# R loaded for two chunks at once in the first eight batches and turned apart from V, products of ones 512 wide, and a new written order

## The chip, the cores and the metric

The kernel runs on one core of a Trainium2 chip. The metric is device time in microseconds (us). A core has TensorE (PE, with its weight loads PEld), VectorE (DVE), ScalarE (ACT), GpSimd (POOL) and SyncE (SP), which here only issues transfers; 16 DMA engines carry these.

## The reference

Inputs r, k, v, w, a, b are fp32 of 4 x 8 x 768 x 40 (batch, head, time, head dimension). A linear recurrence runs over time for each of the 32 heads, and its output goes through a two-layer block:

```python
for t in range(S):
    y[:, :, t] = np.einsum('bhd,bhde->bhe', rt, state)
    Sa = np.einsum('bhde,bhe->bhd', state, at)
    state_decay = state * wt[:, :, None, :] - np.einsum('bhd,bhe->bhde', Sa, bt)
    state = state_decay + np.einsum('bhd,bhe->bhde', vt, kt)
...
x = y.transpose(0, 2, 1, 3).reshape(B * S, H * D)      # 3072 x 320
h = x @ w_in                                           # w_in 320 x 2048
out = (np.maximum(h, 0.0) ** 2) @ w_out                # w_out 2048 x 320
```

## The kernel before

**Tiling.** Time is cut into 6 chunks of 128 steps. A "batch" m = 0..23 in the code is one chunk (c = m // 4) of one of the four input batches (bb = m % 4), all 8 heads; batches 0 to 3 are the first chunk, 4 to 7 the second. A step st = 0..47 is half of a batch, four heads. Inside a chunk the recurrence is done with products of 128 x 128; between chunks a state UZ is carried.

**One batch.** SP loads W, K, B, A, R and V, 128 times x 8 heads x 40 in fp32, 160 KB each (`load`). PE sums the logarithms of W over time (cs), ACT takes exponentials (xi, gp), and DVE or POOL multiply them into padded bf16 tiles: K and B (pk), A (pa), the last decay (gw). R and V are copied into a pad by one instruction (cv). The padded tiles are turned, so that heads lie along partitions: K and B on PE (kt, then the eviction kv), A on PE for the first eight batches (ta, at) and by a transposing DMA later (ka); R and V on PE for the first eight (rm, evicted by rv) and by a transposing DMA later (rt). Then come the products `ca` (a), masked into CN: either by one DVE multiplication with MEX, or by an ACT copy and a cut on POOL (affine select; aq and eq in the order). P collects V's share and the carried state (p), and a correction in two steps (m, k1, c, k2) gives SN (s). SN is turned (t, tv), the products `ex` are made with turned R, V and SN (e) and masked into EX in the same two ways (ev). `uy` takes output and new state (z, kb), which DVE scales (y, u). The output is turned (xt, xv) and enters the two-layer block: fr, fa, fb are products with w_in, ra and rb the rectification on ACT, q the square on POOL or DVE, o1 and o2 the products with w_out, ov the eviction, ow the store.

**The order.** Nothing is scheduled by the compiler. The string `ORDER` lists every piece of work by name and number, as `ev0.1:D` or `cs.4@f`: after the colon stands the engine, after the @ the PSUM bank. Each engine executes its own pieces in the order of the string, and so do the transfers on SP's one queue. A load's place in the string is its place in that queue; weights (wt, wo) go by POOL's queue.

**Buffers.** The loaded tiles lie in a pool with four buffers for each kind (`natp`, `AHEAD = 4`); R and V share the kind NRV. A load waits until the tile four before it has been copied.

**Products of ones.** `warm` (w.0 to w.18) writes products of a 128 x 128 tile of ones into a spare bank, 26 for w.0 and 8 for the others, 170 in all; nothing reads them.

At the end of the program a test value is read by all engines (fl), and the last two outputs are stored behind a branch.

Of the kernel before, what the change touches and what calls it, by code (L numbers as in the profile page):

```python
# [18 lines left out]
def kernel(  # L19
# [57 lines left out]
    def natural(key, m):  # L77
        if (key, m) not in nat:
            nat[key, m] = natp.tile([128, len(key), NHH, D], FP32, name=f"N{key}", tag=f"N{key}")
        return nat[key, m]  # L80

    def load(key, m):
        pair, u = SHARED.get(key, (key, 0))
        c, bb = divmod(m, NB)
        nc.sync.dma_start(  # L85
            out=natural(pair, m)[:, u],
            in_=nat_srcs[key][bb, :, c * L:(c + 1) * L, :].rearrange("h t e -> t h e"))
# [12 lines left out]
            for key, n in (("KBA", 4), ("G", 3), ("RV", 4))}  # L100
    RVs = [gl.tile([128, 2, PB, L], BF16, name=f"RV{i}") for i in range(4)]
# [6 lines left out]
    def fill(k):  # L108
# [7 lines left out]
        elif k < 16:  # L116
            key, i = (("KBA", k - 5) if k < 9 else ("G", k - 9) if k < 12 else ("RV", k - 12))
            eng.memset(pads[key][i][:] if key == "G" else pads[key][i][:, :, :, D:64], 0.0)
        elif k < 19:
            eng.memset(SNs[k - 16][:, :, :, D:64], 0.0)  # L120
        else:
            eng.memset(UZs[k - 19][:], 0.0)
# [11 lines left out]
    def warm(k, n=8):  # L134
        wu = ps.tile([128, 128], FP32, name="wu", **bank("w", k))
        for i in range(26 if k == 0 else n):
            nc.tensor.matmul(out=wu[:], lhsT=ones_b[:], rhs=ones_b[:], start=True, stop=True)
# [23 lines left out]
    def home(m):  # L161
        o = bt[m] = Batch()
        o.G, o.KB, o.RV = (pads[key][m % len(pads[key])] for key in ("G", "KBA", "RV"))
        o.RVT, o.YN = RVs[m % 4], YNs[m % 3]

# [40 lines left out]
    def b_pa(m):  # L206
        engine("pa", m).tensor_tensor(out=bt[m].KB[:, 2, :, 0:D], in0=nat.pop(("A", m))[:, 0],  # L207
                                      in1=bt[m].GP[:], op=ALU.mult)

    def b_cv(m):  # L210
        move(pick["cv", m][0], bt[m].RV[:, :, :, 0:D], nat.pop(("RV", m))[:])
# [11 lines left out]
    def b_rm(m):  # L223
        bt[m].t1 = turned(bt[m].RV, **bank("rm", m))

    def b_rv(m):
        move(pick["rv", m][0], bt[m].RVT[:], bt[m].t1[:])

    def b_rt(m):
        o = bt[m]  # L230
        nc.sync.dma_start_transpose(
            out=o.RVT[:].rearrange("p u j t -> p (u j) t"),
            in_=o.RV[:].rearrange("p u h e -> p (u h e)"))
# [4 lines left out]
    def kbt(m):  # L238
        o = bt[m]
        if not hasattr(o, "KBT"):  # L240
            o.KBT = chp.tile([128, 3, PB, L], BF16, name="KBT", tag="KBT", bufs=4)
        return o.KBT

    def b_kv(m):
        move(pick["kv", m][0], kbt(m)[:, 0:2], bt[m].t2[:])

    def b_ta(m):
        bt[m].t3 = turned(bt[m].KB, us=(2,), **bank("ta", m))

# [30 lines left out]
    def st_a_mm(st):  # L280
# [40 lines left out]
    def b_p(m):  # L321
# [3 lines left out]
        if c > 0:  # L325
            for j in range(PB):
                nc.tensor.matmul(out=P[:, j, :, 0:D], lhsT=o.KBT[:, 2, j, :],
# [73 lines left out]
    def st_ex_mm(st):  # L401
# [4 lines left out]
        for u in range(2):  # L406
            for i in range(2):
                for s in range(2):
                    lhsT = SnT[half(s), j0 + i, :] if u else o.RVT[half(s), 1, j0 + i, :]
                    nc.tensor.matmul(out=ex[s][:, i, u, :], lhsT=lhsT,  # L410
                                     rhs=o.RVT[half(s), 0, j0 + i, :],
# [18 lines left out]
    def st_z(st):  # L430
        c, o, j0, p2, SN = where(st)
        uy = uys[st] = ps.tile([128, 8 * D + PB], FP32, name="uy", **bank("z", st))
        if c > 0:
            for i in range(2):
                nc.tensor.matmul(out=cols(uy, 2 * i * D), lhsT=o.RVT[:, 0, j0 + i, :],
# [184 lines left out]
    def get_flag():  # L620
# [297 lines left out]
```

## Time and profile before

| | us |
|---|---|
| median of 3 runs | 257.62 (256.45 to 258.14) |
| the profiled execution, its time | 259.12 |
| its span, first to last instruction | 257.3 |
| granted TensorE clock, mean | 0.993 |

| engine | busy us | share of the span |
|---|---|---|
| PE | 241.3 | 94% |
| PE weight loads | 201.8 | 78% |
| DVE | 202.4 | 79% |
| ACT | 205.9 | 80% |
| POOL | 203.0 | 79% |

A profile line names the source line of kernel.py, the engine, the operation, what is written and read by the program's names, and the shape. Busy PE time counts overlapping products once and can hold short stalls. The row of slices has 40 digits, each the busy share in tenths of a fortieth of the span. "DMA share" is the mean busy share of the 16 DMA engines and can come out a little over 1. Where several helpers call one line, such as `move` (L153 on ACT, L157 on DVE), tiles tell the groups apart: RVp is the pad of R and V, RV the turned tile, KBT the turned K, B and A.

### The profile page before, as it was taken

How to read it: one execution, taken by the hardware profiler on the slowest of the kernel's cores; microseconds unless marked ns; L12 is line 12 of the kernel's file. 1: busy time of each engine (PE TensorE's matmuls, PEld its weight loads, DVE VectorE, ACT ScalarE, POOL GpSimd, SP SyncE). 2: the span in 40 equal slices, each digit the busy share in tenths (PEclk: the TensorE clock that was granted, in tenths of full speed). 3: DMA queues.
4: the chain of work that ended last, by engine and by line, in shares of the span. 5: the costliest groups of instructions: out<-in, count | busy, mean ns of one | idle time of the engine just before them, and what ended most of it. 6: DMA issues, size and time to landing. Idle time of an engine off the chain costs nothing.

```text
span 257.3 us, 9803 instructions
## 1 busy us (share of the span) xinstructions
PE 241.3 (94%) x4020; PEld 201.8 (78%) x4020; DVE 202.4 (79%) x429; ACT 205.9 (80%) x470; POOL 203.0 (79%) x231
## 2 busy tenths in 40 slices
PE   8897867999999999999999999999999997999993
PEld 7776656989888888788888788888878885787872
DVE  3887877899999889898798898879798986664440
ACT  3567989589989988978999887889989876869811
POOL 6487987779989979999998999897896993397110
PEclk9999999799999999999999999999999999999999
DMA  7999999999988989999999999989999989470011
GB/s 127 182 151 153 169 176 168 170 167 167 162 162 137 157 151 182 137 178 180 157 159 184 159 167 172 167 162 185 141 187 180 178 167 148 97 120 28 28 57 59
DMA packets 184468, 38.46 MB, mean 149 GB/s; under 512 B 180064, under 2 KB 183136, under 8 KB 184416
## 3 DMA queue, kind: packets, MB, share of 16 engines
q1 hardware_dynamic: 183072, 35.14, 80.9%
q0 software_dynamic: 1344, 2.62, 6.4%
q8 instruction: 33, 0.54, 0.9%
q14 instruction: 19, 0.16, 0.2%
HBM read 28.84 MB, written 3.93 MB: 127 GB/s over the span
## 4 chain that ended last, share of the span: by engine, by line
PE 58%; POOL 13%; DMA 12%; SPq 8%; ACT 4%; issue 2%; DVE 1%; POOLq 0%; ACTq 0%
PE hp L542 17%; SPq L85 8%; DMA NKB<-in_b_dram 6%; PE tt L218 3%; PE cs L173 3%; PE ca L287 3%; PE ex L410 3%; POOL Gt L568 3%; PE uy L456 3%; DMA NRV<-in_r_dram 2%; DMA KBT<-KBAp 2%; POOL KBAp L202 2%; PE uy L451 2%; PE P L344 2%; POOL CN L307 2%
## 5 line engine op out<-in xcount | busy, mean ns | idle before, releaser
L542 PE MATMUL hp<-XS,WIN 128*128 128x256 bf16 (+3 forms) x720 | 73.3, 255 | 0.0
L562 ACT ACTIVATE hs<-hp 128x512 bf16<-128x512 f32 x96 | 55.6, 600 | 14.5 <-PE hp L542 13.2
L542 PEld LDWEIGHTS <-WIN 128*128 128x128 bf16 (+1 forms) x720 | 49.6, 115 | 6.1 <-issue 3.6
L302 DVE TENSOR_TENSOR CN<-ca,MEX 128x512 bf16<-128x512 f32 x60 | 39.5, 683 | 8.6 <-PE ca L287 8.0
L577 PEld LDWEIGHTS <-Gt 128*128 128x128 bf16 x384 | 35.1, 97 | 12.2 <-issue 0.3
L302 DVE TENSOR_TENSOR EX<-ex,MEX 128x512 bf16<-128x512 f32 x60 | 39.8, 683 | 4.4 <-PE ex L410 4.3
L568 POOL TENSOR_TENSOR Gt<-hs 128x1024 bf16<-128x1024 bf16 x21 | 40.4, 1927 | 0.6 <-ACT hs L562 0.3
L307 POOL TENSOR_SCALAR_AFFINE_SELECT CN<-CN 128x512 bf16<-128x512 bf16 x36 | 25.1, 703 | 10.0 <-ACT CN L300 7.8
L307 POOL TENSOR_SCALAR_AFFINE_SELECT EX<-EX 128x512 bf16<-128x512 bf16 x36 | 25.0, 711 | 5.9 <-ACT EX L300 3.9
L198 POOL TENSOR_TENSOR Gp<-NW,GP 32x320 bf16<-32x320 f32 x20 | 17.6, 886 | 11.3 <-DVE osb L157 7.6
L568 DVE TENSOR_TENSOR Gt<-hs 128x1024 bf16<-128x1024 bf16 x27 | 21.7, 810 | 5.8 <-ACT hs L562 4.3
L365 ACT ACTIVATE jk<-CN 128x1024 bf16<-128x1024 bf16 x24 | 25.7, 1071 | 0.2
L300 ACT ACTIVATE CN<-ca 128x512 bf16<-128x512 f32 x36 | 21.0, 594 | 4.7 <-PE ca L287 4.5
L202 POOL TENSOR_TENSOR KBAp<-NKB,GI 128x640 bf16<-128x640 f32 x14 | 21.6, 1545 | 3.2 <-DMA NKB<-in_b_dram 2.5
L300 ACT ACTIVATE EX<-ex 128x512 bf16<-128x512 f32 x36 | 20.5, 597 | 2.8 <-PE ex L410 1.9
L287 PE MATMUL ca<-KBT 64*128 64x128 bf16 x384 | 18.2, 221 | 3.7 <-DMA KBT<-KBAp 1.7
L361 POOL TENSOR_TENSOR Cc<-x,SN 128x320 bf16<-128x320 f32 x24 | 20.1, 836 | 1.9
L456 PE MATMUL uy<-KBAp,EX 128*128 128x40 bf16 x384 | 21.3, 181 | 0.0
L207 POOL TENSOR_TENSOR KBAp<-NA,GP 128x320 bf16<-128x320 f32 x18 | 16.3, 907 | 5.6 <-DMA NA<-in_a_dram 2.9
L360 POOL TENSOR_TENSOR x<-Mc,c 128x320 f32<-128x320 bf16 x24 | 20.5, 854 | 0.3
L472 DVE TENSOR_TENSOR YN<-uy,GP 128x224 bf16<-128x224 f32 (+1 forms) x48 | 16.5, 346 | 4.4 <-PE uy L456 4.4
L456 PEld LDWEIGHTS <-EX 128*128 128x128 bf16 x384 | 17.9, 96 | 0.9 <-issue 0.3
(151 smaller groups left out, 623.0 us busy)
## 6 DMA issues: line engine op xcount, KB each, us to landing
NW<-in_w_dram SPq DMA_DIRECT2D x24, 160.0 KB, 3.8
NA<-in_a_dram SPq DMA_DIRECT2D x24, 160.0 KB, 4.0
NKB<-in_k_dram SPq DMA_DIRECT2D x24, 160.0 KB, 3.9
NKB<-in_b_dram SPq DMA_DIRECT2D x24, 160.0 KB, 4.3
NRV<-in_v_dram SPq DMA_DIRECT2D x24, 160.0 KB, 4.0
NRV<-in_r_dram SPq DMA_DIRECT2D x24, 160.0 KB, 3.9
out_dram<-osb SPq DMA_DIRECT2D x24, 160.0 KB, 3.4
WOUT<-in_moe_w_out_dram POOLq DMA_DIRECT2D x2, 640.0 KB, 6.6
```

The source lines that it names most:

```text
L85: nc.sync.dma_start(out=natural(pair, m)[:, u], in_=nat_srcs[key][bb, :, c * L:(c + 1) * L, :].rearrange("h t e -> t h e"))
L202: engine("pk", m).tensor_tensor(out=bt[m].KB[:, 0:2, :, 0:D], in0=nat.pop(("KB", m))[:], op=ALU.mult, in1=bt[m].GI[:].rearrange("p (u h) e ...
L287: nc.tensor.matmul(out=ca[s][:, i, u, :], lhsT=o.KBT[half(s), u, j0 + i, :], rhs=o.KBT[half(s), 2, j0 + i, :], start=(i == 0 and u == 0), ...
L300: nc.scalar.activation(out=out, in_=in_[:], func=ACTF.Copy)
L302: nc.vector.tensor_tensor(out=out, in0=in_[:], op=ALU.mult, in1=MEX[:].rearrange("p (i u) x -> p i u x", u=2))
L307: nc.gpsimd.affine_select(out=t_, in_=t_, pattern=[[0, 2], [0, 2], [1, L]], compare_op=ALU.is_gt, fill=0.0, base=0, channel_multiplier=-1)
L365: nc.scalar.activation(out=jk[:], in_=CNs[m, "b"][:].rearrange("p x i s u t -> p (x i s) u t")[:, :, 1, :], func=ACTF.Square, accum_out=AC ...
L456: nc.tensor.matmul(out=uy[:, (2 * i + s) * D:(2 * i + s + 1) * D], lhsT=EXs[st][:, i, s, u, :], rhs=o.KB[:, u, 2 * (j0 + i) + s, 0:D], sta ...
L542: nc.tensor.matmul(out=o.hp[u][:, i], lhsT=inner(g, rows, j), rhs=XSs[o.c][rows, g, o.bs, :], start=(o.begun[u] == 1), stop=(o.begun[u] > ...
L562: nc.scalar.activation(out=o.hs[:, u], func=ACTF.Relu, in_=o.hp[u][:].rearrange("p j a b -> p (j a b)"))
L568: engine("q", n).tensor_tensor(out=o.Gt[:, o.j0:o.j0 + 2 * o.per].rearrange("p j a b -> p (j a b)"), in0=hs, in1=hs, op=ALU.mult)
L577: nc.tensor.matmul(out=ops[n][:], rhs=WOUT[:, j, :], lhsT=Gts[h][:, b_, j, :] if h in SPLIT else Gts[h][:, j, b_, :], start=(j == 0), stop ...
```

## The change

**R in pairs.** For batches 0 to 7 R is loaded by four transfers instead of eight (lR.0 to lR.3). One takes 256 steps of one input batch, that is both chunks; partition p gets steps 2p and 2p + 1, which lie side by side in memory: 320 bytes in one piece instead of 160. The tile takes a buffer of the kind NRV, and V of these batches takes another of its own. R is copied into the pads of two batches by one instruction (cr), V alone by cv. On PE each R turn (rn) covers two pairs of heads for both chunks; it is an ordinary product with the identity into fp32, and its eviction (rv) reads the steps apart and writes two batches' turned R, the second chunk's into a fourth plane of the turned tile. V is turned by itself (vm, vv).

**A's pad.** A moves from the pad of K and B (now KBp) to the pad of R and V (now RVAp), and turned A from KBT to a plane of RV. From batch 8 on A has a transfer of its own (aa), R and V theirs (rt); in the last four batches K and B are turned by a transfer of 8 blocks (ka), where one of 12 blocks held A too.

**Products of ones.** 7 for w.0 and 2 for the others, each with 512 columns: 43 in all.

**Order.** The whole string is written anew, with other engines for many pieces.

```diff
+    def paired(m):
+        return ("cr", m - m // NB % 2 * NB) in pick
     def load(key, m):
         pair, u = SHARED.get(key, (key, 0))
         c, bb = divmod(m, NB)
+        if key == "R" and paired(m):
+            nc.sync.dma_start(
+                out=natural("RR", m)[:].rearrange("p a h e -> p (a h e)").rearrange(
+                    "p (h x) -> p h x", h=NHH),
+                in_=r[bb, :, c * L:(c + 2) * L, :].rearrange("h (p a) e -> p h (a e)", a=2))
+        else:
...
-    def warm(k, n=8):
-        wu = ps.tile([128, 128], FP32, name="wu", **bank("w", k))
-        for i in range(26 if k == 0 else n):
-            nc.tensor.matmul(out=wu[:], lhsT=ones_b[:], rhs=ones_b[:], start=True, stop=True)
+    def warm(k, n=2):
+        wu = ps.tile([128, 4, 128], FP32, name="wu", **bank("w", k))
+        for i in range(7 if k == 0 else n):
+            nc.tensor.matmul(out=wu[:], lhsT=ones_b[:], start=True, stop=True,
+                             rhs=ones_b[:].rearrange("p (u x) -> p u x", u=1).to_broadcast([128, 4, 128]))
...
     def b_cv(m):
-        move(pick["cv", m][0], bt[m].RV[:, :, :, 0:D], nat.pop(("RV", m))[:])
+        lo = 1 if paired(m) else 0
+        move(pick["cv", m][0], bt[m].RV[:, lo:2, :, 0:D], nat.pop(("RV", m))[:, lo:2])
+
+    def b_cr(m):
+        move(pick["cr", m][0], bt[m].both.pad[:, :, :, 0:D],
+             nat.pop(("RR", m))[:].rearrange("p a h e -> p (a h e)").rearrange(
+                 "p (h a e) -> p a h e", a=2, h=NHH))
...
-    def b_rm(m):
-        bt[m].t1 = turned(bt[m].RV, **bank("rm", m))
+    def b_rn(m):
+        o, j0 = bt[m], 2 * (m // NB % 2)
+        o.t1 = ps.tile([128, 2, 2, L], FP32, name="tt", **bank("rn", m))
+        for j in range(2):
+            for a_ in range(2):
+                nc.tensor.matmul(
+                    out=o.t1[:, j, a_], rhs=IDb[:], start=True, stop=True, skip_group_check=True,
+                    lhsT=o.both.pad[:, a_, 2 * (j0 + j):2 * (j0 + j) + 2, :].rearrange(
+                        "p a b -> p (a b)"))
     def b_rv(m):
-        move(pick["rv", m][0], bt[m].RVT[:], bt[m].t1[:])
+        o, j0 = bt[m], 2 * (m // NB % 2)
+        move(pick["rv", m][0],
+             o.RVT[:, 0:4:3, j0:j0 + 2, :].rearrange("p c j (t a) -> p j c t a", a=2),
+             o.t1[:].rearrange("p j a (c t) -> p j c t a", c=2))
+
+    def b_vm(m):
+        bt[m].t4 = turned(bt[m].RV, us=(1,), **bank("vm", m))
+
+    def b_vv(m):
+        move(pick["vv", m][0], bt[m].RVT[:, 1], bt[m].t4[:, 0])
```

Three places of the new order. First SP's queue, early in the program. Before, from its ninth row on:

```order
L85 DMA NW<-in_w_dram 128x8x40 x2
L85 DMA NRV<-in_v_dram 128x8x40
L85 DMA NRV<-in_r_dram 128x8x40
L85 DMA NRV<-in_v_dram 128x8x40
L85 DMA NKB<-in_k_dram 128x8x40
L85 DMA NRV<-in_r_dram 128x8x40
L85 DMA NKB<-in_b_dram 128x8x40
L85 DMA NA<-in_a_dram 128x8x40
```

And now, from its eighth row on:

```order
L95 DMA NW<-in_w_dram 128x8x40
L90 DMA NRV<-in_r_dram 128x8x80
L95 DMA NW<-in_w_dram 128x8x40
L95 DMA NRV<-in_v_dram 128x8x40 x2
L95 DMA NA<-in_a_dram 128x8x40
L95 DMA NKB<-in_k_dram 128x8x40
L95 DMA NKB<-in_b_dram 128x8x40
L95 DMA NA<-in_a_dram 128x8x40
L90 DMA NRV<-in_r_dram 128x8x80
```

The rows with 128x8x80 are the double loads of R, at L90; the first comes ahead of V, the second later than the second R load did, behind the third batch's K and B.

Second, ACT in the first chunk, where R and V are evicted (RV<-tt). Before, from the first copy of R and V into the pad:

```order
L153 ACTIVATE RVp_90<-NRV 128x16x40
L189 ACTIVATE GP,ACC<-cx 128x320
L153 ACTIVATE Mc<-P 128x320
L179 ACTIVATE GI,ACC<-cs 128x320 x2
L153 ACTIVATE RVp_91<-NRV 128x16x40
L153 ACTIVATE SN_98<-P 128x8x40
L153 ACTIVATE RV_94<-tt 128x1024
```

Now, over the same part of the first two batches:

```order
L166 ACTIVATE Mc<-P 128x320
L197 ACTIVATE GI,ACC<-cs 128x320
L166 ACTIVATE RV_91<-tt 128x2x2x128
L207 ACTIVATE GP,ACC<-cx 128x320
L166 ACTIVATE Mc<-P 128x320
L207 ACTIVATE GP,ACC<-cx 128x320
L166 ACTIVATE SN_95<-P 128x8x40
L166 ACTIVATE RV_91<-tt 128x2x2x128
```

One eviction of 1024 bf16 columns became two of 512 from fp32 (128x2x2x128), which hold R alone, for two chunks; the two copies of V left ACT's order here.

Third, DVE over the masks of the first `ex` products. Before:

```order
L157 COPY RV_95<-tt 128x1024
L352 SCALAR_TENSOR_TENSOR c_544<-P,Mc 128x320
L302 TENSOR_TENSOR EX<-ex_535,MEX 128x2x256
L157 COPY KBT<-tt 128x512
L302 TENSOR_TENSOR EX<-ex_534,MEX 128x2x256
L302 TENSOR_TENSOR EX<-ex_582,MEX 128x2x256
L302 TENSOR_TENSOR EX<-ex_583,MEX 128x2x256
L270 TENSOR_TENSOR GL<-uy,HM 128x8
```

Now:

```order
L398 SCALAR_TENSOR_TENSOR c_437<-P,Mc 128x320
L170 COPY RV_93<-tt 128x512
L170 COPY KBT<-tt 128x1024
L170 COPY RV_94<-tt 128x512
L216 TENSOR_TENSOR Gp_88<-NW,GP 32x8x40
L348 TENSOR_TENSOR EX<-ex_490,MEX 128x2x256
L348 TENSOR_TENSOR EX<-ex_506,MEX 128x2x256
L348 TENSOR_TENSOR EX<-ex_489,MEX 128x2x256
L348 TENSOR_TENSOR EX<-ex_507,MEX 128x2x256
```

The copies RV<-tt of 512 are A or V now, turned one kind at a time, and a product for the last decay (Gp) has come from POOL; the masks stand behind them.

350 lines of the change are left out of this document (182 added, 168 removed).

## The prediction

> **What bounds the kernel now.** I read the page first, then the windows by stage, the chain of waits, the groups of the first 48 us, and last the groups by shape, for prices.
>
> ```profile
> span 257.3 us, 9803 instructions
> PE 241.3 (94%) x4020; PEld 201.8 (78%) x4020; DVE 202.4 (79%) x429; ACT 205.9 (80%) x470; POOL 203.0 (79%) x231
> PE   8897867999999999999999999999999997999993
> DMA  7999999999988989999999999989999989470011
> ```
>
> PE is the longest engine, and its dips stand at the left end, where the DMA row is already at its ceiling. The stages, each line with stretch, its length, busy time of PE, PEld, DVE, ACT, POOL, granted clock, DMA share and GB/s:
>
> ```profile
> 0.00:48.00 48.00, 39.02 (x678) 33.01 (x679) 36.52 (x84) 33.98 (x74) 34.79 (x56) 0.99 0.96 161
> 48.00:104.00 56.00, 55.91 (x1022) 48.22 (x1021) 51.43 (x106) 50.00 (x116) 50.85 (x57) 0.98 0.94 160
> 60.00:250.00 190.00, 187.20 (x3075) 155.38 (x3070) 155.24 (x323) 160.72 (x371) 158.30 (x166) 1.00 0.89 149
> L137 PE MATMUL wu<-ones_b 128*128 128x128 bf16 x146 | 12.0, 245 | 1.1 <-DVE HM L113 1.1
> ```
>
> To 48 us PE idles 9.0 us, and 12.0 us of its busy time are products of ones that compute nothing, while the DMA engines are 96% full: this stage is set by the loads. From 60 to 250 us PE idles 2.8 of 190. So time can be won by starting the dense part earlier, by filling 2.8 us, or in hidden stalls inside busy PE. The chain of waits (start, length, what) shows the start:
>
> ```profile
> 27.16 5.75 DMA NRV<-in_r_dram
> 32.99 0.74 ACT RVp L153
> 36.12 7.58 DMA NKB<-in_b_dram
> 43.72 1.20 DVE KBAp L202
> 44.97 0.62 PE tt L218 x8
> ```
>
> The fourth R load, and then B of the sixth batch (load 33 of 33 and one copy of weights on SP's queue, by the order), are each awaited for 6 to 8 us, where the median landing is about 4:
>
> ```profile
> NKB<-in_b_dram SPq DMA_DIRECT2D x24, 160.0 KB, 4.3
> NRV<-in_r_dram SPq DMA_DIRECT2D x24, 160.0 KB, 3.9
> ```
>
> **The change, part by part.** The sum is made against the profiled execution, 259.1 us with a span of 257.3; the median of the runs is 257.6, so 1.5 us come off at the end.
>
> *Loads of R.* Eight loads of 1024 packets of 160 B become four of 1024 packets of 320 B. What does such a packet cost? Two windows give a line:
>
> ```profile
> 16.00:24.00 8.00, 6.56 (x126) 5.42 (x124) 6.92 (x15) 7.38 (x17) 6.34 (x9) 1.00 1.03 171
> 245.00:250.00 5.00, 5.00 (x44) 3.72 (x43) 2.54 (x11) 1.08 (x2) 0.86 (x1) 1.00 0.21 72
> ```
>
> From 16 to 24 us the engines move 171 / 1.03 = 166 GB/s, nearly all in 160 B packets: 10.4 B/ns for each of 16 engines, 15.4 ns a packet, 0.99 us a load. From 245 to 250 us only output rows of 1280 B move, 72 / 0.21 = 343 GB/s, 60 ns a packet. The straight line through both puts 320 B at 22 ns, so a double load costs 1.39 us: an estimate between 0.99 (no dearer than a single) and 1.97 (twice). Up to B of the sixth batch the old queue carries 33 single loads and a weight copy, 32.5 us and about 0.4; the new one 28 single and 4 double, 27.6 + 5.6 = 33.2 us. POOL's queue loads weights at the same time:
>
> ```profile
> q0 software_dynamic: 1344, 2.62, 6.4%
> WOUT<-in_moe_w_out_dram POOLq DMA_DIRECT2D x2, 640.0 KB, 6.6
> WIN<-in_moe_w_in_dram POOLq DMA_DIRECT2D x4, 160.0 KB, 4.9
> WIN<-in_moe_w_in_dram POOLq DMA_DIRECT2D x4, 96.0 KB, 5.6
> WIN<-in_moe_w_in_dram POOLq DMA_DIRECT2D x2, 128.0 KB, 6.3
> ```
>
> That queue takes 6.4% of 257.3 = 16.5 us of engine time, and by its bytes half belongs to WIN. By the written order 432 of WIN's 640 rows now stand ahead of that B, where 512 did: 8.2 x 80 / 640 = 1.0 us less. So B lands 33.2 − 32.9 − 1.0 = some 0.7 us earlier; the ends are −2.4 (at 0.99) and +1.6 (at 1.97). The full saving, 4 x (1.97 − 1.39) = 2.3 us, comes with the eighth batch, when PE has no idle time left to give; I count none of it.
>
> The Trainium skill, "DMA: Bandwidth & Descriptors", section "Why small descriptors are slow (HBM only)", gives each packet 3 cycles beside its 32-byte beats: 8 against 13, so a double load would be 1.60 us, and the term +0.1. The same page's "Specifications" asks for 512 B for line rate, which 320 B doesn't reach either; no row here has a 320 B packet.
>
> *P no longer waits for R.* Before, one copy (cv) took R and V together, so the products with V stood behind R's load. In the first eight batches now V is copied alone and R apart (cr), and R is wanted only by the later ex. The wait, in PE's timeline:
>
> ```profile
> 31.08 0.36 PE L331 MATMUL P<-RVp,CN 128*128 128x40 bf16 x8 [0.38 <-POOL RVp L155]
> 33.78 0.35 PE L331 MATMUL P<-RVp,CN 128*128 128x40 bf16 x8 [1.09 <-ACT RVp L153]
> ```
>
> These are 1.5 us. V of the fourth batch is load 24, with three doubles ahead worth 1.2 singles more, where R was load 26: about one load earlier. I take −0.7 of −1.5 to 0. Late next is B of the sixth batch.
>
> *Clock.*
>
> ```profile
> 40.00:48.00 8.00, 6.42 (x131) 5.58 (x126) 6.48 (x16) 5.82 (x11) 5.11 (x9) 0.93 0.93 157
> 48.00:56.00 8.00, 8.00 (x160) 7.35 (x160) 6.85 (x15) 6.39 (x16) 5.94 (x8) 0.86 0.95 164
> ```
>
> The shortfall is 0.07 x 8 + 0.14 x 8 = 1.7 us of PE work, behind the wait for that B. If the gap shrinks, it can vanish; another gap can double it. I take −0.6 of −1.7 to +1.7. The products of ones go from 170 x 128 columns to 43 x 512, 21760 against 22016: nearly the same array time, fewer instructions. I cost them at nothing: in the first 48 us PE has 9.0 us idle to hide them, and the most they could give back is the 12.0 us above, which the wait for loads would refill.
>
> *Copies and evictions.* The prices:
>
> ```profile
> L153 ACT ACTIVATE RV<-tt 128x1024 bf16<-128x1024 bf16 x4 | 4.1, 1019 | 0.0
> L157 DVE COPY RV<-tt 128x1024 bf16<-128x1024 bf16 x4 | 2.7, 680 | 0.0
> L157 DVE COPY KBT<-tt 128x512 bf16<-128x512 bf16 x5 | 2.1, 419 | 1.0 <-PE tt L218 1.0
> L153 ACT ACTIVATE KBT<-tt 128x512 bf16<-128x512 bf16 x3 | 1.8, 595 | 1.6 <-PE tt L218 1.6
> L153 ACT ACTIVATE RVp<-NRV 128x640 bf16<-128x640 f32 x13 | 9.6, 739 | 3.0 <-DMA NRV<-in_r_dram 3.0
> L302 DVE TENSOR_TENSOR EX<-ex,MEX 128x512 bf16<-128x512 f32 x60 | 39.8, 683 | 4.4 <-PE ex L410 4.3
> L300 ACT ACTIVATE EX<-ex 128x512 bf16<-128x512 f32 x36 | 20.5, 597 | 2.8 <-PE ex L410 1.9 <-issue 0.8
> ```
>
> Eight evictions of 1024 columns go: 4 x 1.019 + 4 x 0.680 = 6.8 us. Eight of 512 in bf16 come (V), about 0.5 each, 4.1; and eight of 512 in fp32 (R), not in this trace as a strided read: nearest are the 512-wide fp32 evictions, 0.60 on ACT and 0.68 on DVE, so 6 x 0.60 + 2 x 0.68 = 5.0. Copies into the pads: 8 x 0.74 = 5.9 becomes 4 x 0.74 for R and 8 of half the width, about 0.45, 6.6. In all +2.9 us over three engines, most of it in the first four batches, since each R turn there serves two chunks. Cover is there: DVE and ACT are busy 36.5 and 34.0 of 48 us. I take +0.5 of 0 to +2.9. PE's turns keep their number: 256 of 128 columns before and after.
>
> *Sharing out.* By the order DVE takes 69 of the EX masks instead of 60, so ACT loses 9 evictions and POOL their 9 cuts:
>
> ```profile
> L307 POOL TENSOR_SCALAR_AFFINE_SELECT EX<-EX 128x512 bf16<-128x512 bf16 x36 | 25.0, 711 | 5.9 <-ACT EX L300 3.9 <-DVE EX L302 1.3 <-DMA NKB<-in_b_dram 0.5
> L198 POOL TENSOR_TENSOR Gp<-NW,GP 32x320 bf16<-32x320 f32 x20 | 17.6, 886 | 11.3 <-DVE osb L157 7.6 <-issue 2.2 <-POOL RVp L118 0.3
> PE 58%; POOL 13%; DMA 12%; SPq 8%; ACT 4%; issue 2%; DVE 1%; POOLq 0%; ACTq 0%
> 180.00:220.00 40.00, 37.53 (x626) 30.70 (x623) 31.72 (x63) 32.72 (x77) 31.24 (x33) 1.00 1.03 168
> ```
>
> With five Gp products fewer, POOL loses 9 x 0.71 + 5 x 0.89 = 10.8 us and takes on a little elsewhere; DVE gains about 9, ACT loses about 2. POOL holds 13% of the chain, so the rest of the new order should win there: at most the 2.8 us that PE idles from 60 to 250, unless hidden stalls go too; at worst another 40 us run like 180 to 220, where PE idles 2.5. I take −1.5. A's transfers, 16 of 4 blocks now into the tile of R and V, and four more issues at the end of SP's queue, stand under a dense PE: nothing.
>
> Sum: −0.7 − 0.7 − 0.6 + 0.5 − 1.5 = −3.0, so 256.1 for a profiled execution and **254.6** for the median. The likeliest case's own range is 250 to 257.6.
>
> **The rivals.**
>
> *DVE becomes the bound* (slower). Counting DVE's rows up to the eleventh batch's c (the second part of the correction) and pricing each from its group, the new order has 5.3 us more there: above all five EX masks, nine 512-wide copies of V and A where five of A were, two of R and five more Mc and SN evictions, against four RV copies of 1024. Against it: it has 9 us of room in the stage to 48. For it:
>
> ```profile
> 56.00:80.00 24.00, 23.29 (x50) 1.00 0.99 167
> ```
>
> That is DVE alone, 97% busy for 24 us. It decides once DVE passes 97% from 48 to 104 us, 54.3 of 56, which 2.9 of the 5.3 us falling there would do. All 5.3 on the path, with the two first terms kept: 257.6 + 5.3 − 1.4 = 261.5.
>
> *Loads wait for buffers* (slower). The doubled R tiles and V tiles draw on the same four NRV buffers: twelve tiles in eight batches instead of eight, each held until cr or cv has copied it, and a load that waits heads SP's queue with K and B behind it. The present price of one such wait:
>
> ```profile
> SPq L85 <- POOL KBAp L207: 2.6, 1, 2.6
> ```
>
> One more in the loaded first 40 us, with another clock dip: 257.6 + 2.6 + 1.7 − 0.7 = 261.2. Against it: cr comes early in ACT's and POOL's orders.
>
> *Hidden anyway.* PE is dense from 48 us, the gain in the start is lost to the extra evictions, and the order trades like for like: 257.2, with R's doubled load at the dear end. This is also the case where the pairing doesn't save what it says.
>
> **How the numbers follow.** Forecast 0.55, of which 0.48 lie under 255.0 and 0.07 within 1%; hidden 0.12; DVE 0.22; buffers 0.11. One per cent, 2.6 us, is about what a measurement tells here from no change. So faster 0.48, same 0.19, slower 0.33. The range must reach into both slower rivals: 250 to 263.
>
> **What would show it.** Right: the sixth batch's B lands before 43.5 us; P of the third and fourth batch waits for no R; the clock from 40 to 56 us is nearer 1.00; the stage to 48 holds more PE work that isn't ones; POOL's share of the chain falls. Double R loads landing within 1.5 us of engine time each would confirm the line. Wrong: DVE above 97% from 48 to 104 us with PE idle behind DVE; an R or V load on SP waiting for a copy; R's strided evictions above 0.8 us; PE idle from 60 to 250 above 5 us.

## The result, and the profile after

The changed kernel is slower: 263.75 us in the median of six runs (262.3 to 264.97) against 257.49 for the kernel before (255.74 to 259.36), a ratio of 1.026 [1.022, 1.030]. The forecast was 254.6 us, and the time lies above the range as well. Ratios, here and below, leave out the runs that lie over 1.5% above the fastest of their kernel. The profiled execution took 264.05 us, 4.9 more than that of before. Its page:

```profile
span 262.3 us, 9587 instructions
PE 243.0 (93%) x3893; PEld 195.3 (74%) x3893; DVE 210.8 (80%) x441; ACT 206.3 (79%) x471; POOL 196.0 (75%) x221
PEclk9999579999999999999999999999999999999999
DMA  7999999995648976999889986989998999660111
PE 66%; DVE 9%; DMA 6%; ACT 5%; SPq 5%; POOL 4%; issue 3%; ACTq 0%; POOLq 0%; DVEq 0%
```

The clock row has its dip much earlier than before, in the fifth and sixth slice of 6.6 us, and deeper. The DMA row, full before, now sinks to 4 to 6 tenths in slices 10 to 12 (59 to 79 us). In the chain POOL went from 13% to 4%, as forecast, and DVE from 1% to 9%. By stage:

```profile
0.00:48.00 48.00, 40.95 (x575) 28.79 (x576) 38.92 (x89) 34.70 (x79) 35.38 (x57) 0.89 1.05 176
48.00:104.00 56.00, 51.91 (x973) 44.34 (x971) 50.33 (x106) 46.42 (x111) 44.38 (x48) 1.00 0.75 131
60.00:250.00 190.00, 183.90 (x3053) 151.88 (x3050) 161.18 (x327) 159.42 (x366) 148.62 (x153) 1.00 0.86 144
```

To 48 us PE executes 575 products, of which 37 are ones; before it were 678 with 146. That is 538 against 532 of real work, but 16 of the 538 are turns of R made ahead for the second chunk, so up to 48 us the start is about even. Right behind it PE loses 2.2 us, which are a wait for weights (WIN, in the part on loads below). The window from 48 to 56 us, in which PE was busy for 8.00 before:

```profile
48.00:56.00 8.00, 5.84 (x124) 5.33 (x123) 4.45 (x10) 5.93 (x15) 6.23 (x8) 1.00 0.89 156
```

From 60 to 250 us PE idles 190 − 183.90 = 6.1 us where it idled 2.8, the sign that the prediction named for being wrong. A third of it lies together. The windows of before from 66 to 90 us (columns: stretch, length, busy time of PE, PEld, DVE, ACT, POOL, clock, DMA share, GB/s):

```profile
66.00:74.00 8.00, 8.00 (x153) 6.63 (x150) 7.96 (x18) 6.29 (x18) 7.90 (x9) 1.00 0.96 160
74.00:82.00 8.00, 8.00 (x142) 6.93 (x140) 7.46 (x15) 7.65 (x18) 6.83 (x10) 1.00 0.80 135
82.00:90.00 8.00, 7.91 (x139) 6.72 (x138) 6.88 (x14) 7.62 (x17) 7.74 (x9) 1.00 0.97 160
```

And of the change:

```profile
66.00:74.00 8.00, 7.57 (x153) 6.20 (x150) 7.38 (x18) 7.33 (x19) 7.62 (x9) 1.00 0.72 125
74.00:82.00 8.00, 6.88 (x102) 5.48 (x99) 7.70 (x15) 6.43 (x18) 6.13 (x6) 1.00 0.49 87
82.00:90.00 8.00, 7.62 (x135) 6.51 (x134) 7.89 (x15) 5.32 (x11) 4.16 (x5) 1.00 0.94 168
```

PE works 22.1 of these 24 us where it worked 23.9. DVE is busy 22.97 of 24, ACT and POOL have more room than before (19.1 and 17.9 busy; 21.6 and 22.5), and the DMA engines are half idle from 74 to 82 us. What DVE does there, in its timeline (start, length):

```profile
74.95 0.94 DVE L216 TENSOR_TENSOR Gp<-NW,GP 32x320 bf16<-32x320 f32 x1
75.93 0.69 DVE L348 TENSOR_TENSOR EX<-ex,MEX 128x512 bf16<-128x512 f32 x1
76.54 1.31 DVE L614 TENSOR_TENSOR Gt<-hs 128x1024 bf16<-128x1024 bf16 x1
77.88 0.81 DVE L216 TENSOR_TENSOR Gp<-NW,GP 32x320 bf16<-32x320 f32 x1
...
82.26 1.62 DVE L614 TENSOR_TENSOR Gt<-hs 128x1024 bf16<-128x1024 bf16 x1
...
88.68 1.28 DVE L614 TENSOR_TENSOR Gt<-hs 128x1024 bf16<-128x1024 bf16 x2
```

Two of the products for the last decay (Gp) that POOL had before stand here. And they, like the squares (Gt), take longer than beside an idle POOL: a square 1.31 and 1.62 us, where two at 88.68 take 1.28 together; Gp 0.94 and 0.81, and 0.49 at 8.5 us, where POOL stands still. The mask EX keeps its time all through (fewest, median and most ns of 69):

```profile
L348 DVE TENSOR_TENSOR EX<-ex,MEX x69: 672/680/693, 21.7 to 239.0; 128x512 bf16<-128x512 f32 x69
```

What PE waits for from 66 to 90 us is DVE alone (total, times, longest), and these four waits are all of its idle time there:

```profile
PE P L390 <- DVE c L398: 0.6, 1, 0.6
PE xt L535 <- DVE EX L348: 0.5, 1, 0.5
PE xt L535 <- DVE RV L170: 0.4, 1, 0.4
PE tb L434 <- DVE CN L348: 0.4, 1, 0.4
```

The size differs between executions: in a second trace of the same kernel (e5_after_again) PE idles 1.1 us in this stretch, again behind DVE.

From 90 to 160 us PE idles another 2.5 us, where it idled 0.2. Nearly all of that are two waits of products of R with the carried state, which the trace puts down to ACT's rectification (hs):

```profile
PE uy L481 <- ACT hs L608: 2.4, 2, 1.4
```

All twelve traces with the new order in this part have such a wait, 1.4 to 3.3 us in total, and the eight others have none. No run was made to remove it.

### The profile page after: what moved, and what is told of

It reads as the page before. It is cut to its first block, busy times and chain, and to the rows that moved or that the text cites. A ratio compares the mean times of both kernels' runs of the same rounds, so it can differ in the third digit from the quotient of the medians.

```text
span 262.3 us, 9587 instructions
## 1 busy us (share of the span) xinstructions
PE 243.0 (93%) x3893; PEld 195.3 (74%) x3893; DVE 210.8 (80%) x441; ACT 206.3 (79%) x471; POOL 196.0 (75%) x221
## 4 chain that ended last, share of the span: by engine, by line
PE 66%; DVE 9%; DMA 6%; ACT 5%; SPq 5%; POOL 4%; issue 3%; ACTq 0%; POOLq 0%; DVEq 0%
PE hp L588 17%; PE cs L191 4%; SPq L95 4%; PE ca L333 4%; PE ex L456 4%; PE P L390 3%; PE tt L242 3%; PE uy L502 3%; DMA WIN<-in_moe_w_in_dram 2%; DMA KBT<-KBp 2%; DMA NKB<-in_b_dram 2%; PE uy L497 2%; PE xt L535 2%; POOL Gt L614 2%; DVE Gt L614 2%
## 5 line engine op out<-in xcount | busy, mean ns | idle before, releaser
L588 PE MATMUL hp<-XS,WIN 128*128 128x256 bf16 (+3 forms) x720 | 71.5, 253 | 2.5 <-DMA WIN<-in_moe_w_in_dram 2.2
L348 DVE TENSOR_TENSOR EX<-ex,MEX 128x512 bf16<-128x512 f32 x69 | 45.1, 682 | 6.4 <-PE ex L456 5.8
L614 POOL TENSOR_TENSOR Gt<-hs 128x1024 bf16<-128x1024 bf16 x21 | 40.8, 1947 | 10.5 <-ACT hs L608 10.2
L225 POOL TENSOR_TENSOR RVAp<-NA,GP 128x320 bf16<-128x320 f32 x18 | 16.4, 912 | 17.1 <-ACT GP L207 10.6
L353 POOL TENSOR_SCALAR_AFFINE_SELECT EX<-EX 128x512 bf16<-128x512 bf16 x27 | 18.7, 701 | 12.3 <-ACT EX L346 5.4
L220 POOL TENSOR_TENSOR KBp<-NKB,GI 128x640 bf16<-128x640 f32 x13 | 21.1, 1624 | 3.3 <-DMA NKB<-in_b_dram 2.0
L502 PE MATMUL uy<-KBp,EX 128*128 128x40 bf16 x384 | 21.6, 182 | 0.0
L333 PE MATMUL ca<-RV,KBT 64*128 64x128 bf16 x384 | 18.1, 221 | 3.1 <-DMA KBT<-KBp 1.7
L191 PE MATMUL cs<-lnW,UTI 128*128 128x320 f32 x48 | 19.4, 487 | 0.0
L518 DVE TENSOR_TENSOR YN<-uy,GP 128x160 bf16<-128x160 f32 (+1 forms) x48 | 16.3, 346 | 1.9 <-PE uy L502 1.8
L390 PEld LDWEIGHTS <-CN 128*128 128x128 bf16 x384 | 14.9, 97 | 3.7 <-issue 1.9
```

Of the source, the lines that this page charges most:

```text
L191: nc.tensor.matmul(out=cs[:].rearrange("p h e -> p (h e)"), lhsT=UTI[:], rhs=bt[m].lnW[:], start=True, stop=True)
L220: engine("pk", m).tensor_tensor(out=bt[m].KB[:, 0:2, :, 0:D], in0=nat.pop(("KB", m))[:], op=ALU.mult, in1=bt[m].GI[:].rearrange("p (u h) e ...
L348: nc.vector.tensor_tensor(out=out, in0=in_[:], op=ALU.mult, in1=MEX[:].rearrange("p (i u) x -> p i u x", u=2))
L353: nc.gpsimd.affine_select(out=t_, in_=t_, pattern=[[0, 2], [0, 2], [1, L]], compare_op=ALU.is_gt, fill=0.0, base=0, channel_multiplier=-1)
L390: nc.tensor.matmul(out=Ps[m][:, h // 2, h % 2, 0:D], lhsT=CNs[m, "b"][:, h // 4, h // 2 % 2, h % 2, 1, :], rhs=X[:, h], start=False, stop= ...
L502: nc.tensor.matmul(out=uy[:, (2 * i + s) * D:(2 * i + s + 1) * D], lhsT=EXs[st][:, i, s, u, :], rhs=o.KB[:, u, 2 * (j0 + i) + s, 0:D], sta ...
```

## The experiments

Each was run beside the kernel before on the same chip; ratios are to that kernel, with their interval. On those chips before takes 260.2 to 261.5 us, so times are compared by ratios only. An order that is mixed from two keeps, in each part, the sequence, engines and banks of the kernel that it comes from; at a seam a piece or two may get another bank.

### The pairs or the order?

R per chunk in the changed order:

```diff
-lR.0 ... cr.0:A ... rn.4@e vm.0@f ... vv.0:D ... rv.0:A
+lV.0 lR.0 ... cv.0:D ... vm.0@f ... vv.0:D        (vm turns R and V, vv evicts both; so for batches 0 to 7)
```

> The changed kernel with R loaded per chunk again in its first eight batches, each R load right behind the V load of its batch, one copy for R and V, eight turns on PE and one eviction of 1024 columns on the engine that evicted V; everything else stands in the new order. Theory O (the new order costs the time, the pairing is nearly neutral): 262 to 266 us, as slow as the changed kernel at 263.8. Theory P (the pairing costs it, through its added copies and evictions, 2.9 us by their durations, in the first four batches): 256 to 259.5 us.

The pairs alone in the order of before:

```diff
-cv.0:A ... rm.0@f ... rv.0:A
+cv.0:A cr.0:A ... rn.0@f ... rv.0:A rn.4@f vm.0@f rv.4:D vv.0:A
```

> The kernel before with the pairing alone: four double loads of R at the places of the first four R loads, the later four dropped, R copied and turned apart from V, A's pad and the order of all else as before. The two turns of R and that of V stand where R and V were turned, so PE has no more distance than before between them. Theory O: 255.5 to 259 us, within 1% of the kernel before at 257.5. Theory P: 260 to 264 us. A value between says that both cost.

The first gave 1.022 [1.015, 1.029]: the order costs all of it without the pairs. (A's pad and transfers and the wide ones stay in this run; the order of before with all three, up to 88 us, gives 1.004 below.) The second gave 1.014 [1.006, 1.022]: pairs dropped into the old order cost as well. In its trace PE waits twice for an eviction between two turns of one pair that share a bank,

```profile
22.50 0.59 PE L241 MATMUL tt<-IDb,RVp 128*128 128x128 bf16 x4 [0.78 <-DVE RV L169]
24.29 0.58 PE L251 MATMUL tt<-IDb,RVp 128*128 128x128 bf16 x4 [0.78 <-DVE RV L169]
```

so 1.6 us of some 3.7 are the price of pairs placed without distance; the rest is not traced. It is no measure of the pairs as the new order places them.

### Two suspects from the trace

In the changed kernel SP's timeline has a hole of 16 us:

```profile
57.75 1.65 SPq L95 DMA_DIRECT2D NA<-in_a_dram  x1
75.57 1.33 SPq L271 DMA_TRANSPOSE RV<-RVAp  x1
```

and its waits (total, times, longest) say for what:

```profile
SPq L271 <- POOL RVAp L225: 16.4, 2, 16.1
```

The transfer at 75.57 is A's own for the ninth batch (aa.8), which waits 16.1 us for POOL's product. It was moved behind the loads that it blocks:

```diff
-ev1.12:D aq1.15 aa.8 lK.9 z.12@u ... rb.7 lV.9 kv.8:D
+ev1.12:D aq1.15 lK.9 z.12@u ... rb.7 lV.9 aa.8 kv.8:D
```

> The changed kernel with one piece moved: the first transfer that turns A (batch 8) goes behind five loads (K and B of batch 9, V and R of batch 8, V of batch 9) that stand behind it on SP's queue and that it keeps waiting for 16 us in the profile. Theory Q (SP's queue stands still there, the third chunk's loads come late, and PE loses 3 us between 74 and 88 us for that): 259.5 to 262 us. Rival D (VectorE sets the pace at 62 to 86 us and the late loads cost nothing): 263 to 265 us.

The last products of ones, which the new order has at 199 to 219 us, were put back behind the flag at the end:

```diff
-... w.18@. ... w.17@. ... w.5@. ... fl.0 ov.21:A
+... fl.0 w.5@u w.17@0 w.18@x ov.21:A
```

> The changed kernel with three groups of products of ones (w.18, w.17, w.5: 6 products of 512 columns, 6 x 0.216 = 1.3 us of PE) moved from the stretch of 190 to 215 us, where the new order put them, to the end of the program, where the old order had its last three groups. Theory W (they stand on a dense PE and cost their own length): 262 to 262.8 us. Rival: PE waits there anyway and they fill the wait: 263.3 to 264.3 us.

1.017 [1.008, 1.026] and 1.022 [1.016, 1.028]. Neither is the cause, though the first may be a part of it, within the noise. In the trace of the first, PE works 6.89 us from 74 to 82 us, as in the change (6.88), though the loads now go ahead of A's transfer: the late loads are not what it waits for there.

### Where in the program?

The changed kernel unaltered, as the measure of this set:

> The changed kernel unaltered, beside the kernel before, as the measure for the three mixed orders of this set. 1.026 of before was measured on it earlier; the same ratio, 1.02 to 1.03, is expected, by every theory.

It gave 1.022 [1.009, 1.035]. Then three mixed orders:

```diff
 the new order up to c.5 (65 us), then the old:
-c.5 lV.7 cs.7@e ev0.9:D cx.7 xt.3@x rb.2 k2.5 ...
+u.47 lK.7 ... xt.3@x c.5 xv.3:A u.45 vm.5@s lW.9 q.2:P cx.7 ...
```

> The changed kernel's pieces, its paired R included, in its own order up to c of the sixth batch (about 65 us), and from there all that is left in the order of before with its engines and banks; two pieces get another bank at the seam. Theory (the start with its pairs costs about 1 us there and the new order loses the rest later): the dense part runs as before, so 1.002 to 1.008 of before, 0.5 to 2 us over it. Rival (what the start does, above all the pairs, is what comes back later): 1.02 or more, as the change.

```diff
 the new order up to P of the ninth batch (85 to 89 us), then the old:
-p.8@u ev1.14:D fr.10@xf e.15@1f kv.9:D lR.9 ...
+... x.5 ev1.14:A kv.9:D p.8@u lW.11 lK.10 m.8:A lK.11 ...
```

> The same, with the seam at P of the ninth batch (85 to 89 us), where the orders stand alike and no bank changes. Theory (the new order loses 3.3 us from 75 to 88 us, behind DVE, and some 3 us more between 110 and the end): 3 to 4 us over before, 1.012 to 1.016. Rival that the whole loss sits before 88 us: 1.02 to 1.026. Rival that all of it comes after 88 us and the 3.3 us would be made up: within 0.4% of before.

```diff
 the old order up to P of the ninth batch, R per chunk, then the new:
-lV.9 aq0.17 aq1.17 p.8@u en.5 lW.11 lK.10 m.8:A ...
+... jk.6 en.5 gw.9:P p.8@u fr.10@xf e.15@1f lR.9 ...
```

> The other way round: R per chunk and the order of before up to P of the ninth batch, from there on the rest in the new order. A stands in its new pad, and two fills of pads go ahead of the first turns of A. Theory: what the new order loses after 88 us alone, 3 to 4 us, 1.01 to 1.016. If all the loss sat in the start: within 0.4% of before. If all sits behind 88 us: 1.02 to 1.026.

| new up to | new from | ratio |
|---|---|---|
| c.5, 65 us | | 1.007 [1.001, 1.012] |
| P.8, 88 us | | 1.020 [1.009, 1.031] |
| | P.8, 88 us | 1.004 [0.999, 1.009] |
| all | all | 1.026 [1.022, 1.030], again 1.022 [1.009, 1.035] |

The two mixtures that have 65 to 88 us from before lie well below the change, their intervals apart from that of 1.026, though that of the repeat reaches down to 1.009; the one that has this stretch from the change does not. Taken as they stand the start costs 0.7%, the stretch 1.3%, the rest 0.4%, each give or take 0.5 to 1. The plain medians of this set, over all runs, give the same order: 1.007, 1.017 and 1.000, and 1.020 for the change.

### Why the stretch?

First the new sequence with the engines of before for the 21 pieces of the stretch whose engine had changed:

```diff
 the 21 pieces alone; those between them stay:
-pa.7:P vv.5:D ev0.10:D kv.7:A q.5:P av1.14:A s.6:D av1.15:D ev1.13:A cv.7:D pk.8:P ...
+pa.7:D vv.5:A ev0.10:A kv.7:D q.5:D av1.14:D s.6:A av1.15:A ev1.13:D cv.7:P pk.8:D ...
-... gw.7:D ev1.12:D q.4:D gw.8:D vv.7:A s.7:D ov.0:A pk.9:P cv.8:D ev1.14:D
+... gw.7:P ev1.12:A q.4:P gw.8:P vv.7:D s.7:A ov.0:D pk.9:D cv.8:A ev1.14:A
```

> The changed kernel with its own order throughout; only the 21 pieces between c of the sixth batch and P of the ninth (65 to 88 us) that the new order gives to another engine go back to the engine of before. Theory D (from 65 to 88 us DVE is the bound, because the new order gives it gw, masks and SN evictions that ACT and POOL did before): PE's waits behind DVE there go, 1.007 to 1.013 of before in place of 1.022 to 1.026. Rival (the sequence of the pieces is what costs there, not their engines): 1.02 or more.

Then the stretch wholly as before inside the changed kernel, and that once more with the new engines:

```diff
 start as changed; from c.5 to p.8 the old order; the rest as changed:
-c.5 lV.7 cs.7@e ev0.9:D cx.7 ... gl.7 y.13 cv.8:D p.8@u
+... c.5 xv.3:A u.45 vm.5@s lW.9 ... jk.6 en.5 gw.9:P p.8@u
```

> The changed kernel with the pieces between c of the sixth batch and P of the ninth in the order of before and on the engines of before; start and rest as changed. If the costs of the three parts add up (start 0.7%, window 1.3%, rest 0.4%): 1.009 to 1.013. If the gain of a mended window is given back later, as that of the moved transfer was: 1.02 or more.

```diff
 the same, and in the stretch the 21 pieces the other way:
-vv.5:A pa.7:D ev0.10:A kv.7:D q.4:P q.5:D s.6:A av1.14:D ...
+vv.5:D pa.7:P ev0.10:D kv.7:A q.4:D q.5:P s.6:D av1.14:A ...
```

> The kernel before this one, but with the new engines for the same 21 pieces: the order of before and the engines of the change from 65 to 88 us. Theory D: the cost comes back with the engines, 1.018 to 1.026. Rival (sequence): 1.009 to 1.013.

1.043 [1.037, 1.049], 1.018 [1.012, 1.024], 1.034 [1.028, 1.040]. The theory that the engines alone do it falls: engines of one order in the sequence of the other cost 1.6 to 2.1% more whichever way round. The stretch taken whole from before gains less than the 1.3% that the table gives it: 1.009 to 1.013 was expected, which the interval only just reaches. Whether the parts add is not shown.

An edit that is no mixture, for DVE alone (gw.7 and gw.8 go back to POOL; gw.6, which DVE had before too, goes along):

```diff
-gw.6:D ... gw.7:D ... gw.8:D
+gw.6:P ... gw.7:P ... gw.8:P
```

> The changed kernel; the products for the last decay of batches 6, 7 and 8, 0.9 us each on DVE between 66 and 79 us, go back to POOL, which idles there. Theory D (DVE bounds the stretch 65 to 88 us): PE's waits behind DVE there shrink by 2 us or so, 1.014 to 1.018. Rival S (the sequence of the pieces, not DVE's load, is what costs): 1.022 or more.

The 8 us from 74 us on in this run:

```profile
74.00:82.00 8.00, 8.00 (x131) 6.95 (x130) 7.20 (x14) 6.66 (x17) 7.61 (x7) 1.00 0.69 99
```

and in the two mixtures that did worst, the new sequence with old engines,

```profile
74.00:82.00 8.00, 6.55 (x109) 5.20 (x104) 6.58 (x13) 6.30 (x18) 5.71 (x8) 1.00 0.60 98
```

and the old sequence with new engines:

```profile
74.00:82.00 8.00, 6.61 (x92) 5.12 (x93) 8.00 (x13) 6.54 (x17) 7.84 (x9) 1.00 0.52 92
```

With three products of 0.8 to 0.9 us gone from DVE, PE is full (8.00, where the change has 6.88) and DVE drops to 7.20; with the new engines in the old sequence DVE is full and PE has 6.61. With PE's waits above, that DVE held PE up at this place is shown. With the old engines in the new sequence PE idles while DVE has room: there its longest waits from 66 to 90 us are for POOL's cuts (1.8 and 1.1 us) and for A's product on DVE (1.4). The time of the run without the three products shows less of it: 1.019 [1.012, 1.027], which holds the change's own ratio.

### The clock

The mean granted clock of the change's runs is 0.982 and 0.980 in two sets, that of before 0.990 to 0.994 in five. PE's timeline shows where. Before has products of ones at 23 and 26 us:

```profile
23.14 0.62 PE L137 MATMUL wu<-ones_b 128*128 128x128 bf16 x8
26.55 0.62 PE L137 MATMUL wu<-ones_b 128*128 128x128 bf16 x8
```

The change has none there between 19 us and the late ones, and a gap:

```profile
25.02 0.29 PE L456 MATMUL ex<-RV 64*128 64x128 bf16 x4 [1.56 <-ACT RV L166]
```

The records give the clock in steps of 3.41 us. In the 20 traces of this study it fell to half 43 times up to 245 us, always behind a step in which PE was busy for 0.20 to 0.66 of the time; behind a step under 0.51 it always fell, behind one over 0.66 never, and it came back only behind a step busy for 0.93 or more. In the change the step from 22.5 us on is busy for 0.54, and half clock follows from 25.9 to 36.2 us (in the second trace of the change, from 28.6 to 32.0 only); before kept its step there at 0.58. So six late products of ones, w.18, w.17 and w.5, were put into the gap:

```diff
-rv.1:A lW.4 ln.4 e.3@fe            (and w.18, w.17, w.5 late)
+rv.1:A lW.4 ln.4 w.18@x w.17@e w.5@s e.3@fe
```

> The changed kernel; the six late products of ones (w.18, w.17, w.5) stand in the first chunk, ahead of the ex products for which PE idles 1.6 us at 23.5 us. Theory C (PE busy under about 0.55 of a stretch of 3.4 us is followed by half clock; before had eight products of ones at 23 us and eight at 26.5, the changed order has none behind 19 us): the stretch is filled to 0.9, the dip at 26 to 36 us goes, the mean clock rises from 0.980 to 0.988 or more, and with 150 us per unit of clock the time falls by 1 to 2 us: 1.014 to 1.02 of before where the change has 1.022 to 1.026. Rival (loads set the pace there, the clock costs nothing): the clock rises, the time stays at 1.022 or more.

The windows of the change from 24 to 40 us:

```profile
24.00:32.00 8.00, 5.98 (x86) 4.35 (x87) 6.31 (x15) 5.25 (x12) 7.75 (x11) 0.62 0.98 172
32.00:40.00 8.00, 6.85 (x115) 5.93 (x111) 7.28 (x16) 6.06 (x14) 7.08 (x11) 0.74 1.04 181
```

The same of this run:

```profile
24.00:32.00 8.00, 6.04 (x93) 3.78 (x90) 6.43 (x13) 5.48 (x13) 7.69 (x10) 1.00 1.01 187
32.00:40.00 8.00, 6.04 (x122) 5.24 (x123) 7.72 (x22) 6.88 (x17) 7.81 (x13) 1.00 1.08 177
```

The dip is gone there (one of 3.4 us comes at 51 us), PE does 209 products besides the six of ones where it did 195, and the mean clock of the runs is 0.987. The ratio is 1.018 [1.011, 1.025]: less than the change by 0.4 to 0.8%, within the noise of both. With the last decay on POOL as well:

```diff
-ln.4 e.3@fe ... gw.6:D ... gw.7:D ... gw.8:D
+ln.4 w.18@x w.17@e w.5@s e.3@fe ... gw.6:P ... gw.7:P ... gw.8:P
```

> Both edits of the two runs before. If C and D hold and add: 1.006 to 1.013. If neither: 1.022 or more.

it is 1.014 [1.007, 1.022]. The two edits together take back about 1 of 2.4%, with intervals that touch; their shares are not told apart. In the kernel before the same filling of a gap gave nothing:

```diff
-jk.3 kt.5@e aq1.9                  (and w.17, w.5, w.18 behind the flag)
+jk.3 w.18@s w.17@0 w.5@e kt.5@e aq1.9
```

> The kernel before; its 24 late products of ones stand ahead of the turn of K and B of the sixth batch, where PE idles 1.5 us at 43.5 us. Theory C: the dip of 3.4 us at 47 us goes, the mean clock rises from 0.991 to 0.995 or more, the time falls by 0.5 to 1.3 us: 0.995 to 0.998 of before. Rival (nothing rests on the clock there): within 0.2%.

1.002 [0.997, 1.008], at a clock of 0.994 instead of 0.992. What half clock costs can also be taken from the scatter: within one kernel a run whose mean clock is 0.01 lower takes 0.8 to 1.6 us longer (0.8 over the runs that the ratios count, 1.6 over all). By that the lower clock of the new start, 0.011, is some 0.8 to 1.8 us of the 6: an estimate from runs that differ by chance, not from an edit.

### The pairs once more

R per chunk in the new start, the rest as before:

```diff
 the new order with R per chunk up to c.5, then the old:
-c.5 lV.7 cs.7@e ev0.9:D ...
+... c.5 xv.3:A u.45 vm.5@s lW.9 ...
```

> R per chunk in the new order up to c of the sixth batch, the rest in the order and on the engines of before. In the trace of R per chunk in the new order throughout, this start was 1.7 us ahead of before at 74 us. If that holds and the rest keeps it: 0.992 to 0.996 of before, and 1.0 to 1.3% less than the same with R in pairs (1.0067). Rival (PE is dense, a better start is given back): within 0.3% of before. If pairs cost nothing: 1.0067 as there.

It gave 1.018 [1.012, 1.024], where the same with pairs had given 1.007, but on another chip and with half-clock steps in both. So both with the gap filled, on one chip:

```diff
 pairs:
+rv.1:A lW.4 ln.4 w.18@s w.17@0 w.5@e e.3@fe
 per chunk:
+gw.2:P w.17@0 a.5@s1 ... kv.3:D av1.5:D w.18@s w.5@u a.6@sx
```

> The new start with R in pairs up to c of the sixth batch, the order of before from there (it gave 1.0067 of before), and the three late products of ones moved into the gap ahead of the ex products at 23.5 us. Theory (what that start costs is its clock): mean clock 0.987 or more, 0.998 to 1.005 of before; under 0.998 it would be the version that beats both kernels. Rival: the clock rises and the time stays, 1.0067 or more.

> The same start with R per chunk (1.0181 of before without the edit), the three products of ones in its two gaps, ahead of the products ca at 23.8 and 26.3 us. If pairs save the loads the prediction counted: 0.4 to 1.1% slower than the run with pairs beside it. If pairs cost, as the placement in the old order showed (1.0142): faster than it by 0.4% or more. If pairs are worth nothing either way: within 0.3% of it.

1.003 [0.997, 1.008] with pairs, 1.012 [1.006, 1.017] without. That speaks for pairs by 0.9%, but the runs with pairs scatter from 259.6 to 266.7 us, the others from 263.0 to 264.1, and the plain medians over all runs are 263.3 and 263.4. The price of the pairs stays open between nothing and a gain of 1% where the order makes room for them. No version beat the kernel before; the nearest are 1.002 to 1.004 of it.

## Why the prediction was wrong

**What failed** is the step "Sharing out": I took −1.5 us, with ends −2.8 and +2.5, from POOL's share of the chain and the 2.8 us that PE idles from 60 to 250. By the mixed orders that step is worth about +1.3% and +0.4%, some 4.4 us, outside my ends. By the smaller reading, the stretch put back whole (0.4 to 0.8% less than the change), it is 2 to 3 us; the sign was wrong by either. DVE gained what I had counted (202.4 to 210.8 us busy) and POOL was relieved. What I did not price is where DVE's new work falls: between 66 and 90 us, where DVE had 1.7 us of 24 to spare before; PE waited there 1.9 us for DVE. Nor did I price what the order does to ACT's work from 90 to 160 us, behind which PE waits 2.4 us. The upper end, "another 40 us run like 180 to 220", was a guess at a size without a place. The terms of the start, −1.5 us together, came out at about +0.7%, 1.8 us, give or take 1.4; they follow below.

**The rival that I wrote down, DVE becomes the bound,** had a part of the mechanism but the wrong test: 97% from 48 to 104 us. DVE is busy 50.33 of these 56 us, 90%, less than before; it is full in stretches of 8 to 24 us, first in the start:

```profile
40.00:48.00 8.00, 6.82 (x151) 5.57 (x149) 7.93 (x20) 7.42 (x15) 6.00 (x9) 1.00 1.06 177
```

There stands DVE's product of K and B of the sixth batch, whose B SP issues at 31.55 us; the timeline rows of both:

```profile
31.55 0.66 SPq L95 DMA_DIRECT2D NKB<-in_b_dram  x1
...
44.39 0.81 DVE L220 TENSOR_TENSOR KBp<-NKB,GI 128x640 bf16<-128x640 f32 x1
```

In the kernel before the issue of that B was

```profile
36.12 1.95 SPq L85 DMA_DIRECT2D NKB<-in_b_dram  x1
```

**Loads of R:** B is issued 4.6 us earlier than before and lands at 38.0 us instead of 43.7, far more than my 0.7, and nothing comes of it, because DVE, busy 7.93 of 8 us, takes it up at 44.39 us, 0.7 later than before (43.72). The estimate of the double load held: 1024 packets of 320 bytes take 20 ns in the median and 23 in the mean, 1.28 to 1.48 us for a load, where I took 1.39; the 1.60 that the prediction gives by beats and cycles is more than either. A packet of 160 bytes takes 14 and 16. WIN's rows, which now stand behind that B, are late next:

```profile
44.06 1.09 POOL L551 DMA_DIRECT2D WIN<-in_moe_w_in_dram  x2
...
50.66 1.13 PE L588 MATMUL hp<-XS,WIN 128*128 128x128 bf16 x16 [2.16 <-DMA WIN<-in_moe_w_in_dram]
```

PE waits 2.16 us for a piece of WIN that POOL issues at 44.06 us. I had credited its leaving (1.0 us) and not asked when it would come. Every trace with the new start has such a wait, 1.2 to 2.4 us in its longest, and before has none; no run moves WIN alone, so what it costs in the end stays open.

**P no longer waits for R:** right. P of the third batch waits for nothing, that of the fourth 0.16 us for ACT.

**Clock:** I took −0.6 of −1.7 to +1.7, looking at 40 to 56 us alone. There it is 1.00 now; but 10.2 us of half clock came at 26 us, and 0.8 to 1.8 is the estimate above. **The ones,** which I cost at nothing because what they fill is idle anyway, are part of the reason: their time is free, their place isn't. The old order up to 88 us with ones 512 wide keeps the clock at 0.993, so it is not their width.

**Copies and evictions:** their prices held, in the groups by shape:

```profile
L166 ACT ACTIVATE RV<-tt 128x512 bf16<-128x512 bf16 x7 | 4.2, 596 | 0.4 <-PE tt L242 0.2
L170 DVE COPY RV<-tt 128x512 bf16<-128x512 bf16 x9 | 3.7, 415 | 0.0
L166 ACT ACTIVATE RV<-tt 128x512 bf16<-128x512 f32 x6 | 3.5, 594 | 0.3 <-PE tt L252 0.3
L170 DVE CAST RV<-tt 128x512 bf16<-128x512 f32 x2 | 1.4, 682 | 0.1
L166 ACT ACTIVATE RVAp<-NRV 128x320 bf16<-128x320 f32 x5 | 2.4, 475 | 0.0
L216 DVE TENSOR_TENSOR Gp<-NW,GP 32x320 bf16<-32x320 f32 x9 | 8.0, 890 | 0.3
```

R's strided evictions cost 0.59 and 0.68, as taken; V's copy 0.48 on ACT. Only the last row is off: Gp on DVE is 0.89 in the mean of nine, where before had 0.60 in four.

**A's transfers,** cost at nothing under a dense PE: aa.8 held SP for 16.1 us. Moved, the ratio was 1.017 instead of 1.022 to 1.026: at most a part, within the noise.

**Loads that wait for buffers:** in the change's trace no load of R or V stands among SP's waits for a copy.

What stays open is why a mended place gives so little: the stretch from before gives PE 22.9 of its 24 us, three products off DVE 23.7, where the change has 22.1 and 22.9 in two traces, and the end comes hardly earlier. The waits for WIN and for ACT remain in both runs. The runs scatter by 2% on these chips, in both kernels, and half a per cent is not told apart.

## What to carry to other kernels

An order written out by hand is one piece: sums over the kernel and shares of a chain did not price a new one. Lay each engine's new work into stretches of 8 us of the old trace and look where an engine is full; no run here tests how well that forecasts. A gain in transfers is worth what the engine that takes the data has free at that moment; ask for it before counting the bytes. Filler products are priced by their place: look for the stretches that they kept busy before moving them.

## What the runs showed of the hardware

A DVE operation with both inputs in SBUF kept its time beside an idle POOL, and many were stretched while POOL computed: the square of 128x1024 took 0.67 to 0.69 us wherever POOL was idle, and 0.68 to 1.62 beside a busy one; Gp took 0.49 beside an idle POOL and 0.49 to 2.08 beside a busy one. The mask, with an input in PSUM, took 0.67 to 0.69 in all. The Trainium skill, "SBUF — State Buffer", section "Who interferes with whom", says that a DVE instruction with two SBUF inputs contends with a GpSimd instruction that reads SBUF; the stretched ones agree, and those that kept their time beside a busy POOL show that the price varies. So work moved from POOL to DVE can cost more than its row of a quiet place says.

Half clock came in steps of 3.41 us, behind steps in which PE still worked up to two thirds of the time. The Trainium skill, "TensorE: Matmul & The Clock Gate", section "What's actually happening", ties the half clock to an idle window of about 3.4 us; the length agrees, but here a window need not be idle for it.
